# Attention and two expert layers on one core: three edits around the first pass of the routed experts

## Chip, core and metric

The kernel runs on one core of one Trainium2 chip. The metric is the time of one execution in microseconds (us), as the device measures it, with the median of three runs as the kernel's time. Engines are named as in the profile: PE (TensorE, the matmuls; its weight loads are PEld), DVE (VectorE), ACT (ScalarE), POOL (GpSimd) and SP (SyncE, which here only issues DMAs).

## What is computed

Causal attention over 2 batches of 12 heads (448 tokens of 64 each) gives a matrix x of 896 tokens by 768. A dense layer follows, x @ w_in, a gate h * sigmoid(1.702 h), then @ w_out. Then every token goes to one of 8 experts:

```python
logits = x @ w_gate
e_idx = np.argmax(logits, axis=1)
...
gate_w = probs[np.arange(N), e_idx]
eom = 1.0 / (1.0 + np.exp(-(x @ w_output_gate)))
...
for e in range(E):
    mask = e_idx == e
    h = np.maximum(x[mask] @ w1[e], 0.0)
    ye = h @ w2[e]
    out[mask] = gate_w[mask, None] * eom[mask, e, None] * ye
```

N is 896, D is 768, an expert's inner size is 1024. All inputs are float32.

## The kernel before, in words

The attention and the dense layer fill the first 392 us. Each matmul of the dense and the expert layers is done as a product of split numbers: a float32 weight tile `raw` is cast by ACT to a rounded part `hi`, and DVE makes the rest `lo = raw - hi`. PE then adds hi*hi, hi*lo and lo*hi.

**Expert passes.** A pass (`block`, line 858) takes up to 128 tokens of one expert. It has 12 steps `u`. In steps 0 to 5 (`l1`) PE multiplies the tokens `xh`, `xl` by two 128-row pieces of w1, in steps 6 to 11 (`l2m`) it multiplies the hidden values `hh`, `hl` by pieces of w2: steps with `u % 3 == 2` work on the output's last 256 columns (`pyB`), the others on its first 512 (`pyA`). Between them stand `relu` (ACT, writes `hs`), `tr` (PE transposes `hs`, ACT copies the result to `hh`, DVE makes `hl`), and at the end two scalings by ACT into `ys`, which POOL scatters to the output. `prep` (line 691) makes the next pass's `xh`, `xl` from its gathered tokens `xw`: six transposes on PE, two casts on ACT, two subtractions on DVE.

**Splits.** Each step's weights stand in one of 24 places of 512 KB and are split by `split` (line 292: one ACT cast of some 1.04 us and one DVE subtraction of some 1.22 us) into one of 6 entries, in the order of passes and steps. Five splits (`SPLIT_AT`, line 133) are done while the dense layer's last tile still runs. So at step u of a pass, `split` works on step u + 5, and from u = 7 on the next pass's weights. An entry can be written again when PE is done with the step that used it six splits earlier. When a split of a pass marked `True` in `passes` is done, SP issues the load of the same step's weights of the expert two later (`again`, line 274, `load32`, line 269). Pass 0 is marked `False`: passes 0 and 1 both use expert 0's weights, so pass 0's own splits issue no load. SP issues its DMAs in program order and stands still at the first one whose wait is not fulfilled.

**Where pass 0 and pass 1 get their tokens.** Tokens are sorted into lists in DRAM (`xl_d`), by expert. For each tile of 128 tokens, `logits` and `logits_sum` give the logits, `pick` (line 643) finds the expert and the gate weight, and `place` (line 667) computes each token's position in its expert's list and has POOL scatter the entry `lst[:, t, :]` (token number and gate weight) there. After the first five of seven tiles (`CUT`) the list of expert 0 is read and its tokens are gathered: this is pass 0. The last tile's logits, `pick` and `place` are done inside pass 0. Then POOL reads the rest of expert 0's list (`rest_lists`, line 788: `le0` and the window lists `lwin`), gathers those tokens (`first_x`, line 936), and `prep` makes them ready for pass 1. From pass 1 on the next pass's tokens are gathered early in the pass before.

**Hooks.** `block` is given functions by place: a pair such as (0, 3) runs inside or after an `l1` step of half 0 (an odd second number: after the step that holds that k), a number 6 to 11 after that step's `split`. A function's instructions are queued on each engine at that place of the program, and each engine works in program order.

The program runs 8 experts plus expert 0's second pass, then as many further passes as overfull lists need: twelve passes ran in this execution. After line 939 (the call for pass 0) every other pass is `some(p)`.

## Time and profile before

| | us |
|---|---|
| runs | 633.08, 633.17, 637.72 |
| median | 633.17 |
| the profiled execution | 635.76 |
| its span, first to last instruction | 634.0 |
| PE busy in the span | 592.1 (93%) |
| DVE busy | 470.1 (74%) |
| ACT busy | 372.1 (59%) |
| mean granted clock of PE | 0.978 of full speed |

A row of the timeline gives the start and the duration in us, the engine, the line of the program, the operation, what it writes and reads, shapes, how many instructions were merged, and in square brackets how long the engine was idle before and which event ended that. Pass 0 begins at 393.92 us of the span, pass 1 at 424.97 us, pass 2 at 444.40 us.

### The profile page before, as it was taken

Reading aid. Unit: us, or ns where it says so; the run is one execution under the profiler, and the core shown is the slowest. Engines: PE = TensorE matmul, PEld = TensorE weight load, DVE = VectorE, ACT = ScalarE, POOL = GpSimd, SP = SyncE. Lnnn points to the kernel's source line nnn. Section 1 sums busy time; section 2 is a strip of 40 time slices with the busy share of each in tenths; the row PEclk is TensorE's granted clock in tenths of the full one; section 3 lists DMA queues with packets and bytes.
Section 4 is the critical chain, followed back from the end, with each engine's and each line's share of the span. In section 5 each row is a group of like instructions: output and inputs, shape, how many; then the busy total and the mean of one; then the engine's idle time right before and its main releaser. Section 6 shows DMA issues by size and latency. Waiting matters only on the chain. (4 is left out here: it accounts for less than half of the span.)

```text
span 634.0 us, 10087 instructions
## 1 busy us (share of the span) xinstructions
PE 592.1 (93%) x3326; PEld 477.9 (75%) x3326; DVE 470.1 (74%) x890; ACT 372.1 (59%) x729; POOL 202.4 (32%) x291
## 2 busy tenths in 40 slices
PE   6999999999999979787999999959999999999995
PEld 4666666688888859687877777747888888888884
DVE  2767877467777786877844457839998888898896
ACT  3888888333333324434332225737888888888885
POOL 3354444334333343757400012230551111011110
PEclk8999999999999979998999999979999999999998
DMA  6835552125444443402592305148999999999950
GB/s 138 244 85 142 115 120 62 55 68 144 135 134 138 140 148 100 150 17 81 162 348 36 131 17 174 53 154 273 353 365 353 360 335 383 380 382 381 382 191 20
DMA packets 93144, 118.02 MB, mean 186 GB/s; under 512 B 40206, under 2 KB 53406, under 8 KB 93088
## 3 DMA queue, kind: packets, MB, share of 16 engines
q1 hardware_dynamic: 88560, 109.05, 53.3%
q0 software_dynamic: 2512, 5.54, 2.5%
q10 hardware_dynamic: 2016, 2.75, 1.2%
q8 instruction: 28, 0.46, 0.4%
q14 instruction: 28, 0.23, 0.1%
HBM read 114.10 MB, written 7.54 MB: 192 GB/s over the span
## 5 line engine op out<-in xcount | busy, mean ns | idle before, releaser
L575 PE MATMUL py<-slotA,gs 128*128 128x256 f32 (+1 forms) x609 | 115.2, 343 | 1.3 <-POOL gs L507 1.3
L575 PEld LDWEIGHTS py<-slotA,gs 128*128 128x128 f32 x609 | 93.4, 196 | 14.4 <-issue 2.7
L437 PE MATMUL ph<-xhi,slotA 128*128 128x512 f32 (+1 forms) x384 | 97.5, 373 | 4.7 <-DVE g L536 4.7
L228 POOL TENSOR_TENSOR slotA<-w,slotA 128x512 fp32r<-128x512 f32 x45 | 62.0, 1379 | 81.7 <-ACT slotA L226 81.6
L437 PEld LDWEIGHTS ph<-xhi,slotA 128*128 128x128 f32 x384 | 70.8, 191 | 15.3 <-issue 5.8
L226 ACT CAST slotA<-w 128x512 fp32r<-128x512 f32 x45 | 27.9, 620 | 89.9 <-DVE w L224 89.9
L301 DVE TENSOR_TENSOR ent<-wraw,ent 128x1024 fp32r<-128x1024 f32 x48 | 58.0, 1221 | 4.9 <-ACT ent L300 4.9
L437 PE MATMUL ph<-xlo,slotA 128*128 128x512 f32 x192 | 56.0, 372 | 0.0
L367 PE MATMUL sc<-kT,qz 128*128 128x64 f32 (+6 forms) x168 | 52.6, 397 | 3.0 <-ACT kT L358 2.8
L507 DVE TENSOR_TENSOR gs<-g,gs 128x512 fp32r<-128x512 f32 x38 | 31.5, 837 | 31.8 <-ACT gs L505 31.8
L390 POOL TENSOR_SCALAR P<-P,rc 128x64 f32<-128x64 f32 (+2 forms) x72 | 36.7, 511 | 54.4 <-DVE rc L389 40.5
L875 PE MATMUL ps_h<-ent,xh 128*128 128x512 f32 x192 | 53.9, 402 | 0.0
L224 DVE SCALAR_TENSOR_TENSOR w<-raw,w 128x512 uint32<-128x512 uint32 x46 | 51.9, 1129 | 1.2
L381 ACT ACTIVATE P<-sc,nmax 128x64 f32<-128x64 f32 (+6 forms) x84 | 40.3, 480 | 18.7 <-DVE nmax L379 7.6
L300 ACT CAST ent<-wraw 128x1024 fp32r<-128x1024 f32 x48 | 49.9, 1051 | 0.4 <-ACT y L597 0.4
L379 DVE TENSOR_REDUCE nmax<-sc 128x1 f32<-128x64 f32 (+6 forms) x84 | 34.6, 416 | 16.6 <-PE sc L368 16.4
L536 DVE TENSOR_TENSOR g<-ph,g 128x256 f32<-128x256 f32 x64 | 23.6, 389 | 30.1 <-ACT g L535 30.1
L505 ACT CAST gs<-g 128x512 fp32r<-128x512 f32 x56 | 33.1, 617 | 14.7 <-PE py L575 9.1
L875 PEld LDWEIGHTS ps_h<-ent,xh 128*128 128x128 f32 x192 | 35.0, 188 | 7.3
L398 PE MATMUL ps_pT<-ident,P 128*128 128x128 f32 x192 | 37.7, 289 | 2.2 <-POOL P L390 1.6
L301 DVE TENSOR_TENSOR ent<-wrb,ent 128x1024 fp32r<-128x1024 f32 x30 | 36.3, 1222 | 4.7 <-ACT ent L300 4.2
L221 DVE SCALAR_TENSOR_TENSOR w<-raw,w 128x512 uint32<-128x512 uint32 x46 | 38.0, 827 | 1.6
(190 smaller groups left out, 1211.8 us busy)
## 6 DMA issues: line engine op xcount, KB each, us to landing
wraw<-in_moe_w_dram SPq DMA_DIRECT2D x66, 512.0 KB, 7.8
wrb<-in_moe_w_dram SPq DMA_DIRECT2D x48, 512.0 KB, 8.2
wr<-in_moe_w_dram SPq DMA_DIRECT2D x30, 512.0 KB, 6.2
raw<-in_moe_w_in_dram SPq DMA_DIRECT2D x24, 512.0 KB, 4.3
raw<-in_moe_w_out_dram SPq DMA_DIRECT2D x22, 512.0 KB, 3.6
qraw<-in_q_dram SPq DMA_DIRECT2D x24, 112.0 KB, 2.9
kraw<-in_k_dram SPq DMA_DIRECT2D x24, 112.0 KB, 2.9
vraw<-in_v_dram SPq DMA_DIRECT2D x24, 96.0 KB, 2.5
```

The costliest lines, as they stand in the source:

```text
L221: nc.vector.scalar_tensor_tensor(wu, r[:, :, 1], 0xC0000000, wu, op0=ALU.bitwise_and, op1=ALU.bitwise_or)
L224: nc.vector.scalar_tensor_tensor(wu, r[:, :, 0], 29, wu, op0=ALU.logical_shift_right, op1=ALU.bitwise_or)
L228: nc.gpsimd.tensor_sub(slot[:, 1], w, slot[:, 0].bitcast(F32))
L300: nc.scalar.copy(hi, raw)
L301: nc.vector.tensor_sub(lo, raw, hi.bitcast(F32))
L367: nc.tensor.matmul(sc[:, :n], qT[:, j].rearrange("d h p -> d (h p)"), kT[:, :n], start=True, stop=False)
L381: nc.scalar.activation(Pb[j][:, :n], sc[:, :n], AF.Exp, bias=nm, scale=1.0, accum_out=sm)
L390: eng[NORM_ENG[j]].tensor_scalar(Pb[j][:, :n], Pb[j][:, :n], rc, 1.0, op0=ALU.mult, op1=ALU.mult)
L398: nc.tensor.transpose(ps[:, c].rearrange("p h q -> p (h q)"), Pb[j][:, c * KC:(c + 1) * KC], ident)
L437: nc.tensor.matmul(p[:, 0:128 * nt], wt, xt[:, kk, 128 * t0:128 * (t0 + nt)], start=kk == 0 and n == 0, stop=kk == KD - 1 and n == 2)
L575: nc.tensor.matmul(py[:, :n], gt[:, kk % 4], wt, start=kk == 0 and m == 0, stop=kk == KF - 1 and m == 2)
L875: nc.tensor.matmul(hps[hf], xh[:, k0 + n], wt[:, n], start=k0 + n == 0 and m == 0, stop=False)
```

## The change

Four things change, all for pass 0:

1. `pick` of the last tile stops after the expert is known (`split_off=True`). The seven operations for the gate weight move to `weigh`, which `place` calls after it has computed the positions and before the scatter. For the other tiles the order stays.
2. `block` takes a number of splits for each step (`rate`). Pass 0 has none in steps 0 to 2, two each in steps 3 to 5, one each after that. All passes keep twelve.
3. `prep` for pass 1 moves from the hook after step 10 to the one after step 11.
4. `first_x` issues, behind the gather of pass 1's tokens, a DMA of one element of `xw` to DRAM on SP's queue (`gate`), which can be issued only when the gather has landed.

```diff
--- before.py
+++ after.py
@@ -640,7 +640,7 @@
 
         ohs = {}
 
-        def pick(t):
+        def pick(t, split_off=False):
             logits_sum(t)
             lg = lg_t.pop(t)
             nm = mp.tile([128, 8], F32, name="nm", tag="nm", bufs=2)
@@ -655,6 +655,15 @@
             nc.vector.tensor_scalar(nm[:, 2:3], nm[:, 0:1], -1.0, None, op0=ALU.mult)
             nc.scalar.activation(tmp[:, 1], lg[:, 0:NE], AF.Exp, bias=nm[:, 2:3], scale=1.0,
                                  accum_out=nm[:, 4:5])
+            if not split_off:
+                weigh(t, nm, tmp, lg, ohb)
+            else:
+                late_w.append((t, nm, tmp, lg, ohb))
+            ohs[t] = ohb
+
+        late_w = []
+
+        def weigh(t, nm, tmp, lg, ohb):
             nc.vector.tensor_mul(tmp[:, 2], lg[:, NE:2 * NE], ohb)
             nc.vector.tensor_reduce(nm[:, 3:4], tmp[:, 2], axis=AX.X, op=ALU.add)
             nc.scalar.activation(nm[:, 5:6], nm[:, 3:4], AF.Exp, scale=-1.0)
@@ -662,7 +671,6 @@
             nc.vector.tensor_scalar_add(nm[:, 5:6], nm[:, 5:6], 1.0)
             nc.vector.tensor_mul(nm[:, 6:7], nm[:, 4:5], nm[:, 5:6])
             nc.vector.reciprocal(lst[:, t, 1:2], nm[:, 6:7])
-            ohs[t] = ohb
 
         def place(t):
             ohb = ohs.pop(t)
@@ -675,6 +683,8 @@
             nc.vector.tensor_mul(tmp, p[:, 0:NE], ohb)
             nc.vector.tensor_reduce(pos, tmp, axis=AX.X, op=ALU.add)
             nc.vector.tensor_copy(pos_i, pos)
+            while late_w:
+                weigh(*late_w.pop())
             nc.gpsimd.indirect_dma_start(
                 out=xl_d[:, :], out_offset=bass.IndirectOffsetOnAxis(ap=pos_i.bitcast(U32), axis=0),
                 in_=lst[:, t, :].bitcast(I32), in_offset=None, bounds_check=NT * NE - 1, oob_is_err=False)
@@ -855,7 +865,7 @@
 
         npass = [0]
 
-        def block(lw, hooks):
+        def block(lw, hooks, rate=(1,) * NU):
 
             o, last = passes[npass[0]]
             p0 = npass[0]
@@ -906,7 +916,8 @@
                 l1(u)
                 if u % 3 == 2:
                     relu(u // 3)
-                split()
+                for _ in range(rate[u]):
+                    split()
             hook("b")
             pyA = ps.tile([128, 512], F32, name="ps_yA", tag="acc", bufs=4)
             pyB = ps.tile([128, 512], F32, name="ps_yB", tag="acc", bufs=4)
@@ -924,7 +935,8 @@
                     nc.scalar.activation(ys[:, 0:512], pyA, AF.Copy, scale=scl)
                 if u == 11:
                     nc.scalar.activation(ys[:, 512:768], pyB[:, 0:256], AF.Copy, scale=scl)
-                split()
+                for _ in range(rate[u]):
+                    split()
                 hook(u)
             nc.gpsimd.indirect_dma_start(
                 out=out[:, :], out_offset=bass.IndirectOffsetOnAxis(ap=lw[:, 0:1].bitcast(U32), axis=0),
@@ -933,13 +945,16 @@
         engs = (ET.PE, ET.DVE, ET.Pool, ET.Activation, ET.SP)
         lists = [lw0, le0] + [lwin[:, e] for e in ORDER[1:]] + lo_t
 
+        gate = dram.tile([1, 1], F32, name="gate")
+
         def first_x():
             gather(le0, xw)
+            nc.sync.dma_start(gate, xw[0:1, 0:1])
 
         block(lw0, {
-            (0, 1): lambda: tr_y(TT - 1, "A"), (0, 2): last_logits, (0, 3): lambda: pick(TT - 1),
+            (0, 1): lambda: tr_y(TT - 1, "A"), (0, 2): last_logits, (0, 3): lambda: pick(TT - 1, True),
             (0, 5): last_place, (1, 0): rest_lists, (1, 3): first_x, (1, 4): counts, 6: further_constants,
-            10: lambda: prep(xw)})
+            11: lambda: prep(xw)}, (0, 0, 0, 2, 2, 2, 1, 1, 1, 1, 1, 1))
         nov = None
 
         def some(p):
```

On DVE, from the last tile's gate weight to the first `hl` of pass 0. Before (L301 is the subtraction of `split`, L675 to L677 are the positions, L892 is `hl`; L658, L659 and L661 stand ahead of these rows):

```order
L662 TENSOR_SCALAR nm<-nm 128x1
L663 TENSOR_TENSOR nm<-nm 128x1
L664 RECIPROCAL lst<-nm 128x1
L301 TENSOR_TENSOR entb<-wraw,entb 128x1024
L675 TENSOR_TENSOR tmp_4518<-ps_rk,ohb 128x8
L676 TENSOR_REDUCE pos<-tmp_4518 128x1
L677 CAST pos_i<-pos 128x1
L301 TENSOR_TENSOR entb<-wraw,entb 128x1024
L301 TENSOR_TENSOR ent_4300<-wraw,ent_4299 128x1024
L892 TENSOR_TENSOR hl<-ps_hT,hh 128x512
```

After the change (the positions are now L683 to L685, the gate weight L667 to L673, `hl` L902):

```order
L683 TENSOR_TENSOR tmp_4508<-ps_rk,ohb 128x8
L684 TENSOR_REDUCE pos<-tmp_4508 128x1
L685 CAST pos_i<-pos 128x1
L667 TENSOR_TENSOR tmp<-ps_lg,ohb 128x8
L668 TENSOR_REDUCE nm<-tmp 128x1
L670 TENSOR_SCALAR nm<-nm 128x1
L671 TENSOR_SCALAR nm<-nm 128x1
L672 TENSOR_TENSOR nm<-nm 128x1
L673 RECIPROCAL lst<-nm 128x1
L301 TENSOR_TENSOR ent_4343<-wraw,ent_4342 128x1024
L301 TENSOR_TENSOR entb<-wraw,entb 128x1024
L902 TENSOR_TENSOR hl<-ps_hT,hh 128x512
```

The subtraction that stood between the gate weight and the positions is gone, as is one that stood ahead of the logits; both, and the one behind the positions, now follow the gate weight in one row.

On PE, the end of pass 0 and the begin of pass 1. Before (L899 and L901 are `l2m`, L696 the transposes of `prep`, L875 and L879 `l1` of pass 1):

```order
L901 MATMUL ps_yA<-ent_4332,hl 128x512 x2
L696 MATMUL ps_x<-ident,xw_2992 128x128 x6
L899 MATMUL ps_yB<-ent_4342,hh 128x256
L899 MATMUL ps_yB<-ent_4343,hh 128x256
...
L901 MATMUL ps_yB<-ent_4342,hl 128x256 x4
L875 MATMUL ps_h_4686<-entb,xh 128x512 x4
L879 MATMUL ps_h_4686<-entb,xl 128x512 x2
```

After the change:

```order
L911 MATMUL ps_yA<-ent_4332,hl 128x512 x2
L909 MATMUL ps_yB<-ent_4342,hh 128x256
L909 MATMUL ps_yB<-ent_4343,hh 128x256
...
L911 MATMUL ps_yB<-ent_4342,hl 128x256 x4
L706 MATMUL ps_x<-ident,xw_2992 128x128 x6
L885 MATMUL ps_h_4688<-entb,xh 128x512 x4
L889 MATMUL ps_h_4688<-entb,xl 128x512 x2
```

The six transposes of pass 1's tokens have moved behind the twelve matmuls of step 11, directly ahead of pass 1's first step.

On SP, the last weight loads ahead of pass 0 and the first ones inside it. Before:

```order
L272 DMA wraw<-in_moe_w_dram 128x2x512 [waits DMAHW1_49,PE_49]
L272 DMA wraw<-in_moe_w_dram 128x2x512 [waits DMAHW2_49,PE_49,Pool_49]
L272 DMA wraw<-in_moe_w_dram 128x4x256 [waits DMAHW3_49,PE_49,Pool_49]
L272 DMA wr_3651<-in_moe_w_dram 128x2x512 [waits DMAHW5_49,DVE_49]
L272 DMA wr_3653<-in_moe_w_dram 128x2x512 [waits DMAHW6_49,DVE_49]
```

After the change:

```order
L272 DMA wraw<-in_moe_w_dram 128x2x512 [waits DMAHW1_49,PE_49]
L272 DMA wraw<-in_moe_w_dram 128x2x512 [waits DMAHW2_49,PE_49,Pool_49]
L272 DMA wraw<-in_moe_w_dram 128x4x256 [waits DMAHW3_49,PE_49,Pool_49]
L952 DMA gate<-xw_2992 1x1 [waits DMAHW5_49,DMASW3_49]
L272 DMA wr_3651<-in_moe_w_dram 128x2x512 [waits DMAHW6_49,DVE_49]
L272 DMA wr_3653<-in_moe_w_dram 128x2x512 [waits DMAHW7_49,DVE_49]
```

The DMA of `gate` waits for the software DMA's semaphore (the gather), and the loads that pass 0's last five splits issue stand behind it.

## Rows read from the trace of the kernel before

**Rows 1.** Stretches: us, busy (instructions) of PE, PEld, DVE, ACT, POOL, clock, DMA, GB/s

```profile
425.00:445.00 20.00, 19.43 (x102) 16.10 (x102) 16.74 (x28) 15.86 (x21) 2.52 (x2) 0.98 0.77 247
521.00:540.00 19.00, 19.00 (x103) 16.07 (x102) 16.89 (x18) 15.55 (x21) 2.96 (x3) 1.00 1.05 383
```

**Rows 2.** Timeline of PE, pass 0 to the begin of pass 1

```profile
400.16 0.18 PE L670 MATMUL ps_rk<-ohb,sut 128*128 128x8 bf16 x1
...
402.59 0.66 PE L889 MATMUL ps_hT<-ident,hs 128*128 128x128 f32 x4 [0.72 <-ACT hs L883]
...
421.10 1.51 PE L696 MATMUL ps_x<-ident,xw 128*128 128x128 f32 x6 [7.51 <-DMA xw<-y_d,le]
...
426.68 1.09 PE L875 MATMUL ps_h<-entb,xh 128*128 128x512 f32 x4
...
428.08 1.09 PE L875 MATMUL ps_h<-ent,xh 128*128 128x512 f32 x4
```

**Rows 3.** Waits, 386 to 426 us: us in total, times, longest

```profile
PEld ps_lg L638 <- DVE lT L633: 0.5, 1, 0.5
```

**Rows 4.** Timeline of DVE in pass 0

```profile
401.52 0.17 DVE L664 RECIPROCAL lst<-nm 128x1 f32<-128x1 f32 x1
402.08 1.23 DVE L301 TENSOR_TENSOR entb<-wraw,entb 128x1024 fp32r<-128x1024 f32 x1 [0.39 <-ACT entb L300]
...
403.61 0.15 DVE L677 CAST pos_i<-pos 128x1 int32<-128x1 f32 x1
...
404.83 1.22 DVE L301 TENSOR_TENSOR ent<-wraw,ent 128x1024 fp32r<-128x1024 f32 x1
405.96 0.68 DVE L892 TENSOR_TENSOR hl<-ps_hT,hh 128x512 fp32r<-128x512 f32 x1
406.57 1.22 DVE L301 TENSOR_TENSOR ent<-wraw,ent 128x1024 fp32r<-128x1024 f32 x1
...
407.97 1.23 DVE L301 TENSOR_TENSOR ent<-wraw,ent 128x1024 fp32r<-128x1024 f32 x1
```

**Rows 5.** Timeline of ACT in pass 0

```profile
401.02 1.03 ACT L300 CAST entb<-wraw 128x1024 fp32r<-128x1024 f32 x1
401.95 0.59 ACT L883 ACTIVATE hs<-ps_h 128x512 f32<-128x512 f32 x1
402.44 1.04 ACT L300 CAST entb<-wraw 128x1024 fp32r<-128x1024 f32 x1
...
413.62 0.69 ACT L924 ACTIVATE hs<-ps_yA,lw 128x512 f32<-128x512 f32 x1 [1.59 <-PE ps_yA L901]
```

**Rows 6.** Timeline of POOL: scatter of the last list, its rest, pass 1's tokens

```profile
404.04 1.73 POOL L678 DMA_INDIRECT xl_d<-lst,pos_i  x1 [9.80 <-DVE pos_i L677]
...
409.36 1.90 POOL L724 DMA_INDIRECT le<-xl_d,ix  x1 [3.47 <-DMA xl_d<-lst,pos_i]
...
413.46 1.81 POOL L686 DMA_INDIRECT xw<-y_d,le  x1 [1.22 <-issue]
```

**Rows 7.** DMA issues: count, KB where known, us from issue to landing

```profile
lo<-xl_d,ix POOLq DMA_INDIRECT x6, 6.5
...
xw<-y_d,lw POOLq DMA_INDIRECT x1, 4.6
le<-xl_d,ix POOLq DMA_INDIRECT x1, 3.3
...
xw<-y_d,le POOLq DMA_INDIRECT x1, 7.5
```

**Rows 8.** Timeline of SP's queue: weight loads after pass 0's splits

```profile
412.09 16.24 SPq L272 DMA_DIRECT2D wr<-in_moe_w_dram  x5
```

**Rows 9.** Timeline of PE in the dense layer, after a pause

```profile
268.77 0.64 PE L627 MATMUL ps_lT<-yT,wg 128*32 128x128 f32 x4 [2.34 <-DVE yT L617]
```

**Rows 10.** Stretches of one us, PE: busy (instructions), clock, DMA share, GB/s

```profile
268.00:269.00 1.00, 0.23 (x4) 0.82 0.48 193
425.00:426.00 1.00, 1.00 (x5) 0.67 0.00 0
```

## Prediction, written before the changed kernel ran

> **What bounds the kernel now.** I read the waits of PE first, then stretches of the span, then the timelines of PE, DVE, ACT, POOL and SP around pass 0. From pass 1 on PE is the bound: it is busy 19.43 of 20 us in pass 1 and 19.00 of 19 in a later stretch, where DVE has 16.89, ACT 15.55 and the granted clock is 1.00 [rows 1]. So whatever moves the begin of pass 1 moves the end by as much, as long as nothing new is late behind it. The one long wait of PE near the edits is ahead of pass 1: 7.51 us until pass 1's tokens landed [rows 2]. PE stood still from 413.59, came back at 421.10 at the lower of its two clock levels (1.2 of 2.4 GHz), and the clock rose within the microsecond 425 to 426, which has a mean of 0.67, so about 425.7 [rows 10]. The first step of pass 1 that ran at full clock begins at 426.68, and one step takes 428.08 - 426.68 = 1.40 us [rows 2]. **At full clock pass 1 would thus have begun at 426.68 - 1.40 = 425.28**; against this I count.
>
> The wait is the end of a chain: positions done (DVE, 403.61), scatter issued (404.04), landed and the rest of the list read (409.36), tokens gathered (413.46) [rows 4, 6], landed 7.5 us later [rows 7].
>
> **The change, part by part: the tokens.** Between the gate weight (ends 401.52 + 0.17 = 401.69) and the positions stand a wait of 0.39 for ACT and a subtraction of `split` that holds DVE 1.14 us [rows 4]. Both go: the last of the nine small operations starts at 403.61 - 1.53 = 402.08. Further ahead, the subtraction of step 0 leaves too. It held the logits' add, for which PE's next weight load waited 0.5 us [rows 3]; PE has own work in half of that, so I take 0.24 (bounds 0 and 0.5). Putting the positions ahead of the gate weight is worth nothing by itself: the scatter sends the token number and the gate weight together, so it starts behind both in either order. It only fills time in which DVE waits for ACT's exponential; I take 0.2 (0 to 0.5). Last operation: 402.08 - 0.24 - 0.2 = 401.64; the scatter follows 0.43 later as before [rows 4, 6]: 402.08, **1.96 us earlier** (1.5 to 2.5). From there I keep the distances, 5.32 us to the list and 4.10 us to the gather [rows 6], since nothing else moves data there: gather issued at 411.50.
>
> It took 7.5 us while SP issued five weight loads from 412.09 on [rows 8]. Now those stand behind `gate`. What a quiet queue gives isn't in the trace for this gather. The nearest rows: the list read takes 3.3 us here and 6.5 in the loaded passes, 3.2 us apart; pass 0's gather took 4.6 [rows 7]. I take 7.5 - 3.2 = 4.3, close to that 4.6; bounds are 3.3 and the old 7.5. **Tokens land at 415.8** (414.8 to 419.0), not at 421.0.
>
> **DVE.** The three splits that leave steps 0 to 2 come back in steps 3 to 5. ACT's `relu` of the first half no longer waits behind a cast that ran from 401.02 to 401.95 [rows 5]; it starts some 0.1 us behind the exponential of the gate weight, at 401.14, 0.81 earlier. The first cast follows 0.49 later (402.44 - 401.95), and its subtraction 1.06 after that (402.08 - 401.02) [rows 4, 5]: DVE starts its splits at 402.69. From there it has seven of pass 0 and five of pass 1, two `hl` and the counts, without a pause: a subtraction holds it 405.96 - 404.83 = 1.13 us, an `hl` 0.61, the counts 407.97 - 406.57 - 1.13 = 0.27 [rows 4]. That is 12 x 1.13 + 2 x 0.61 + 0.27 = 15.05 us, to 417.74. So DVE becomes the tight engine of pass 0; before, it had those three splits out of the way early.
>
> **PE.** The transposes of the first half move with `relu`, from 402.59 [rows 2] to 401.78. Then come 0.4 for them, steps 4 and 5 (1.5 each), 6, 7, 8 (1.4 each), transposes of the second half (0.35) and the first four of the six matmuls of step 9 (two thirds of 1.40, 0.93): 410.8. These are estimates from the step of 1.40 and from 0.66 for four transposes, of which the next work hides a part [rows 2]. There the second `hl` is wanted, which stands behind seven subtractions, the first `hl` and the counts: 402.69 + 7.91 + 0.61 + 0.27 + 0.68 = 412.16. **A new wait of 1.4 us.** Then 0.5, and steps 10 and 11 with 1.4 and 1.5: PE is done with pass 0 at 415.6. Step 11 is so taken ahead of the wait; before, it ran behind it, at half clock.
>
> **Begin of pass 1.** Tokens (415.8) and PE (415.6) meet. But `prep` now stands behind the scaling and the split of step 11 on ACT: scaling at 415.95 (some 0.35 behind PE; the scaling of step 10 started 0.03 behind PE's end [rows 2, 5], so this is the cautious end), cast at 416.3, first cast of `xh` 0.95 later (401.95 - 401.02 = 0.93 for a cast [rows 5]), done 417.75. PE starts at 417.8; on DVE the last subtraction starts at 417.36, the first `xl` is ready at 419.05, and PE wants it 0.93 us into the step: 0.3 us of waiting. Effective begin 418.1. The tokens have 0.9 us to spare.
>
> **The sum:** 425.28 - 418.1 = 7.2 us. From the profiled execution's 635.76 that gives 628.6; it lies 2.59 above the median of the runs, so I forecast 633.17 - 7.2 = **626.0**. Costed at nothing: the DMA of `gate` itself (one element; SP has only loads behind it); the loads it holds, four or five of the five in rows 8, until about 416.5. They are pass 3's weights, so all of pass 1 (19.43 us) and more covers them; if that cover were gone, the splits would wait, and PE behind them, as long as the hold lasts, some 4.5 us.
>
> **Rivals.** *The clock falls in the new pauses.* A pause of 2.34 us was enough in the dense layer [rows 9]: the granted clock's mean in that microsecond was 0.82 [rows 10], between the two levels. Here there are 1.4 us at 411 and 2.2 at 416, the latter broken by six transposes. Against it: each is shorter than 2.34. Before, the low level lasted from 421.10 to 425.7, 4.6 us; at half rate that costs 2.3, part of it in the pause; I take 1.8. Gain 5.4, time **627.8**.
>
> *The gather stays at 7.5.* Pass 0's gather had loads beside it and took 4.6 [rows 7]; that the other one was slow because of loads is not shown. It would land at 419.0, after a pause of 3.4, so with the clock down: first `xh` 1.4 us later as before, 420.5, and half rate until 4.6 us after the restart, 423.7, loses 1.6. Effective begin 422.1, gain 3.2, time **630.0**. The Trainium skill, "DMA: Bandwidth & Descriptors", section "Queues, rings and completion order", speaks for this one: an engine takes turns between the queues that have work, a packet at a time, so a gather should not stand behind whole loads of SP's queue, and holding them back would buy little. The list reads of 3.3 and 6.5 us [rows 7] rather agree with a queue that is waited for; I give the rule less weight than these.
>
> *DVE and ACT are less tight.* Then PE's 415.6 decides, plus some 1.1 for the first three transposes and a cast, 416.7: gain 8.6, time **624.6**.
>
> *Slower.* The held loads come as one burst when pass 2's gather is issued, and the DMA engines never catch up: in the later stretch they are full (share 1.05, 383 GB/s [rows 1]). A load is 0.524 MB, 1.37 us at 383 GB/s. If each of the ten gathers of passes 2 to 11 landed one load too late for PE, that costs 13.7 against the gain of 7.2: **639.7**. It decides from 0.72 us a pass. Against it: in pass 1 the share is 0.77 with 247 GB/s [rows 1]; the spare 136 GB/s take in four loads (2.1 MB) in 15 us, less than a pass.
>
> **How the numbers follow.** Forecast 0.50 (its own range 624.9 to 627.1: the scatter's bounds and a few tenths of waiting), clock 0.18, gather 0.14, less tight 0.08, gain lost in small waits (around 632) 0.04, slower 0.06. The range runs from 623.8, below the case with the least waits, to 630.3, above the slow gather. A measurement here tells about 1% from no change; 1% faster is below 626.84. That holds for most of the forecast's case (0.43), the less tight one (0.08) and the cheap end of the clock's (0.03): 0.54. Slower 0.06, the rest 0.40.
>
> **What would show it.** The scatter at about 402.1; the gather's landing in 4 to 5 us; a wait of PE for `hl` at step 9 of 1 to 2 us; no wait of PE for the tokens above 1 us; pass 1 begins at 417 to 418.5 at clock 1.00; DVE without a gap from 402.7 to 419; pass 1 and later as long as before. The forecast is wrong if the gather's time does not fall, if the clock is 0.5 in pass 1's first steps, or if PE waits in later passes.

## The result

The changed kernel takes 629.13 us (median of 7 runs, 628.62 to 629.49); the kernel before took 635.85 us beside it (7 runs, 633.08 to 637.72). The ratio is 0.9902 with a 95% interval of 0.9878 to 0.9925, that is 4.8 to 7.8 us of 635.85. The forecast was 626.0, range 623.8 to 630.3: the time lies inside, 3.1 us above the forecast, and the gain is just short of the 1% to which I had given 0.54.

Span to span, the profiled executions stand at 634.0 and 626.8 us: 7.2 us, the size that was forecast. Nearly all of it arises in pass 0. From pass 0's first matmul to the begin of pass 1 at full clock it was 425.28 - 393.92 = 31.36 us; now it is 24.27. From pass 2's first matmul to the end it was 634.0 - 444.40 = 189.6 us; now it is 626.8 - 437.21 = 189.6.

PE's timeline of the changed kernel, from step 9 of pass 0 to the second step of pass 1 (L909 and L911 are `l2m`, L706 the transposes of `prep`, L885 and L889 `l1`):

```profile
412.02 0.74 PE L911 MATMUL ps_yA<-ent,hl 128*128 128x512 f32 x2 [1.19 <-DVE hl L902]
...
415.38 0.82 PE L706 MATMUL ps_x<-ident,xw 128*128 128x128 f32 x6
417.53 1.20 PE L885 MATMUL ps_h<-entb,xh 128*128 128x512 f32 x4 [1.33 <-ACT xh L708]
418.88 0.73 PE L889 MATMUL ps_h<-entb,xl 128*128 128x512 f32 x2
419.44 1.09 PE L885 MATMUL ps_h<-entb,xh 128*128 128x512 f32 x4
```

The pause of 7.51 us [rows 2] is gone. In its place stand 1.19 us for `hl` at step 9 and 1.33 us for `xh`. The tokens are not waited for. Pass 1's first step starts at 417.53; its last two matmuls come 0.4 us late (418.88 instead of 417.53 + 0.93), so the second step starts at 419.44 and the begin at full clock is 419.44 - 1.40 = 418.04.

The clock in that stretch (PE busy, granted clock, DMA share, GB/s):

```profile
411.00:412.00 1.00, 0.00 (x0) 1.00 0.00 0
...
416.00:417.00 1.00, 0.20 (x2) 1.00 0.39 45
417.00:418.00 1.00, 0.47 (x2) 1.00 0.80 268
418.00:419.00 1.00, 0.85 (x5) 1.00 0.94 346
```

It stays at 1.00 through both pauses. In the kernel before it had fallen to 0.50 inside the long one:

```profile
419.00:420.00 1.00, 0.00 (x0) 0.50 1.06 407
```

POOL, DVE, ACT and SP of the changed kernel, as rows 4 to 6 and 8 show them of before, and the gather of pass 1's tokens among the DMA issues:

```profile
402.42 0.98 POOL L688 DMA_INDIRECT xl_d<-lst,pos_i  x1 [8.29 <-DMA xl_d<-lst,pos_i]
...
406.85 1.75 POOL L734 DMA_INDIRECT le<-xl_d,ix  x1 [3.34 <-DMA xl_d<-lst,pos_i]
...
410.90 1.39 POOL L696 DMA_INDIRECT xw<-y_d,le  x1 [1.32 <-PE ps_yA L909]
```

```profile
401.37 0.16 DVE L673 RECIPROCAL lst<-nm 128x1 f32<-128x1 f32 x1
402.41 1.27 DVE L301 TENSOR_TENSOR ent<-wraw,ent 128x1024 fp32r<-128x1024 f32 x1 [0.87 <-ACT ent L300]
...
411.28 0.68 DVE L902 TENSOR_TENSOR hl<-ps_hT,hh 128x512 fp32r<-128x512 f32 x1
...
418.27 1.02 DVE L709 TENSOR_TENSOR xl<-ps_x,xh 128x384 fp32r<-128x384 f32 x2
```

```profile
400.75 0.20 ACT L669 ACTIVATE nm<-nm 128x1 f32<-128x1 f32 x1 [0.78 <-DVE nm L668]
400.86 0.58 ACT L893 ACTIVATE hs<-ps_h 128x512 f32<-128x512 f32 x1
...
416.05 1.04 ACT L300 CAST ent<-wr 128x1024 fp32r<-128x1024 f32 x1
416.99 0.87 ACT L708 CAST xh<-ps_x 128x384 fp32r<-128x384 f32 x2
```

```profile
415.04 0.31 SPq L952 DMA_DIRECT2D gate<-xw  x1
415.45 3.30 SPq L272 DMA_DIRECT2D wr<-in_moe_w_dram  x5
```

```profile
xw<-y_d,le POOLq DMA_INDIRECT x1, 4.1
```

Step by step: the gate weight's last operation (L673) starts at 401.37; the scatter at 402.42 [404.04 in rows 6]; the gather at 410.90 [413.46]; it lands 4.1 us later [7.5 in rows 7], and SP's `gate` follows at 415.04 with the five loads behind it. DVE starts the first split (L301) at 402.41 and comes to the second `hl` (L902) only at 411.28, to pass 1's `xl` (L709) at 418.27. ACT casts `xh` (L708) at 416.99, directly behind the cast of the last split at 416.05.

### The profile page after: what moved, and what is told of

Its sections match the earlier page's. It is cut to its first block, busy times and chain, and to the rows that moved or that the text cites. A ratio compares the mean times of both kernels' runs of the same rounds, so it can differ in the third digit from the quotient of the medians.

```text
span 626.8 us, 10089 instructions
## 1 busy us (share of the span) xinstructions
PE 590.7 (94%) x3326; PEld 476.2 (76%) x3326; DVE 470.1 (75%) x890; ACT 371.3 (59%) x729; POOL 200.3 (32%) x291
## 5 line engine op out<-in xcount | busy, mean ns | idle before, releaser
L301 DVE TENSOR_TENSOR ent<-wraw,ent 128x1024 fp32r<-128x1024 f32 x48 | 58.0, 1222 | 5.7 <-ACT ent L300 5.7
L885 PE MATMUL ps_h<-ent,xh 128*128 128x512 f32 x192 | 54.0, 402 | 0.0
L224 DVE SCALAR_TENSOR_TENSOR w<-raw,w 128x512 uint32<-128x512 uint32 x46 | 52.0, 1131 | 1.2
L300 ACT CAST ent<-wraw 128x1024 fp32r<-128x1024 f32 x48 | 49.8, 1050 | 0.0
L885 PEld LDWEIGHTS ps_h<-ent,xh 128*128 128x128 f32 x192 | 35.0, 188 | 7.6 <-DVE ent L301 0.4
L301 DVE TENSOR_TENSOR ent<-wrb,ent 128x1024 fp32r<-128x1024 f32 x30 | 36.3, 1222 | 4.7 <-ACT ent L300 4.2
L437 PEld LDWEIGHTS ph<-xlo,slotA 128*128 128x128 f32 x192 | 35.5, 191 | 4.7
```

The lines of the kernel that those rows point to most:

```text
L224: nc.vector.scalar_tensor_tensor(wu, r[:, :, 0], 29, wu, op0=ALU.logical_shift_right, op1=ALU.bitwise_or)
L300: nc.scalar.copy(hi, raw)
L301: nc.vector.tensor_sub(lo, raw, hi.bitcast(F32))
L437: nc.tensor.matmul(p[:, 0:128 * nt], wt, xt[:, kk, 128 * t0:128 * (t0 + nt)], start=kk == 0 and n == 0, stop=kk == KD - 1 and n == 2)
L885: nc.tensor.matmul(hps[hf], xh[:, k0 + n], wt[:, n], start=k0 + n == 0 and m == 0, stop=False)
```

## The experiments

Executions differ in when pass 0 begins (393.4 to 395.4 us in the profiles below), which lies ahead of everything that the change touches. So the kernels are compared by the time from pass 0's first matmul to pass 2's first matmul, in each kernel's profile; "gather" is pass 1's gather, from issue to landing. Medians and ratios are those of the timed runs, against runs of the kernel before on the same chip; different kernels ran on different chips, so two medians are compared only where the text says that the chip was the same.

| kernel | pass 0 | pass 2 | between | gather | median | ratio to before, interval |
|---|---|---|---|---|---|---|
| before | 393.92 | 444.40 | 50.48 | 7.5 | 635.85 | |
| changed | 393.77 | 437.21 | 43.44 | 4.1 | 629.13 | 0.9902, 0.9878 to 0.9925 |
| changed, no hold | 394.21 | 437.58 | 43.37 | 4.2 | 628.84 | 0.9928, 0.9900 to 0.9956 |
| changed, `prep` at step 10 | 393.92 | 436.49 | 42.57 | 4.6 | 627.89 | 0.9907, 0.9882 to 0.9933 |
| changed, gate weight first | 393.38 | 436.43 | 43.05 | 4.1 | 628.48 | 0.9925, 0.9899 to 0.9952 |
| changed, even splits | 395.17 | 439.34 | 44.17 | 4.8 | 630.79 | 0.9961, 0.9943 to 0.9978 |
| before + hold | 394.38 | 441.73 | 47.35 | 4.4 | 632.88 | 0.9988, 0.9968 to 1.0009 |
| before + `prep` at step 11 | 394.42 | 441.34 | 46.92 | 5.5 | 632.88 | 0.9982, 0.9956 to 1.0008 |
| before + positions first | 394.26 | 441.64 | 47.38 | 6.0 | 632.93 | 0.9973, 0.9948 to 0.9998 |
| before + splits moved | 395.02 | 437.26 | 42.24 | 4.4 | 628.64 | 0.9923, 0.9900 to 0.9945 |
| changed, other numbers of splits | 395.35 | 436.96 | 41.61 | 3.9 | 627.69 | 0.9907, 0.9873 to 0.9942 |
| the same, gate weight first, no hold | 393.54 | 434.80 | 41.26 | 4.2 | 627.75 | 0.9904, 0.9876 to 0.9932 |
| changed + second hold | 394.26 | 437.61 | 43.35 | 4.1 | 628.88 | 0.9916, 0.9883 to 0.9949 |
| before + one split earlier | 393.97 | 441.31 | 47.34 | 5.8 | 634.50 | 1.0008, 0.9986 to 1.0029 |

Where no landing is printed, the table has another time. With the hold it is the time from the gather's issue to that of `gate` on SP, which elsewhere follows the landing by 0.1 us or less (410.57 to 415.17 with `prep` at step 10, 413.57 to 418.36 with even splits). For "before + splits moved" it is the time from the issue at 411.72 to PE's transposes at 416.12, for which PE waited.

One thing has to be kept in mind with the first row: the profiled execution of the kernel before, with 635.76 us, is slow for its kind: four sets of 10 to 21 runs of it have medians of 633.38 to 634.07. Four kernels whose runs differ from those of before by 0.3% or less (hold, late `prep`, positions first, one split earlier) have 46.92 to 47.38 us in this column, not 50.48. So differences to 50.48 probably overstate what an edit gives.

The theory from the prediction: the token chain comes forward, the hold makes the gather short, and then DVE's and ACT's row of splits binds pass 1. The rivals: the gather is short for another reason; the single edits do nothing or harm.

### The changed kernel without the hold

```diff
             gather(le0, xw)
-            nc.sync.dma_start(gate, xw[0:1, 0:1])
```

> The changed kernel without the DMA of gate, so the loads of pass 0's last five splits are issued as soon as their places are free. In the changed kernel the tokens land at 415.0 us and the first cast of xh starts at 417.0, so the tokens have some 1.5 us to spare. Theory A (loads slow a gather only while both are in flight): the first of these loads is issued behind the subtraction that ends at about 413.1, 1 us after the gather's descriptors are written; the gather takes 4.1 to 5.5 us, pass 1 begins where it did, time within 0.5 us of the changed kernel. Theory B (the hold is what makes the gather short): 7.5 us, tokens at 418.4, first xh near 419.4, pass 1's effective begin 420 or later: 2 to 4 us slower than the changed kernel.

SP's queue, POOL's gather and its landing:

```profile
413.54 5.63 SPq L272 DMA_DIRECT2D wr<-in_moe_w_dram  x5
```

```profile
411.28 1.44 POOL L696 DMA_INDIRECT xw<-y_d,le  x1 [2.41 <-PE ps_yA L909]
```

```profile
xw<-y_d,le POOLq DMA_INDIRECT x1, 4.2
```

The gather is as short without the hold, 4.2 us, and the stretch is 43.37 us against 43.44. The first load is issued at 413.54, 0.8 us behind the end of POOL's instruction for the gather (411.28 + 1.44 = 412.72). In the kernel before three of the five loads were issued ahead of that end: it was at 413.46 + 1.81 = 415.27 [rows 6], the first load at 412.09 [rows 8]. So once the splits are moved, no load stands ahead of the gather for the hold to keep back. Both sides have moved: counted from pass 0's first matmul, the end of the gather's instruction came 2.84 us sooner than in the profile of before (18.51 against 21.35), the first load 1.16 us later (19.33 against 18.17). Theory A.

### The kernel before with the hold alone

```diff
             gather(le0, xw)
+            nc.sync.dma_start(gate, xw[0:1, 0:1])
```

> The kernel before with the DMA of gate behind pass 1's gather and nothing else of the change. From the first matmul of pass 0 to pass 1's begin at full clock (second step minus 1.40) the kernel before takes 31.36 us, the changed one 24.27; without the hold the changed one also takes 24.26. Theory A (here the five loads are in flight with the gather, from 412.09 on, so the hold matters where the splits stay): the gather takes 4.1 to 4.8 instead of 7.5, PE's pause shrinks to 4 to 4.7 us, the clock still falls as the pause is over 2.3: 27.5 to 28.5 us, 3 to 4 us faster than before. Theory B (an engine takes turns between queues, loads do not hold a gather up): the gather stays near 7.5, no change.

PE's wait for the tokens with the second step of pass 1, the gather on POOL, and its landing:

```profile
418.47 1.51 PE L696 MATMUL ps_x<-ident,xw 128*128 128x128 f32 x6 [4.50 <-DMA xw<-y_d,le]
...
424.07 1.10 PE L875 MATMUL ps_h<-entb,xh 128*128 128x512 f32 x4
```

```profile
413.92 1.81 POOL L686 DMA_INDIRECT xw<-y_d,le  x1 [1.22 <-issue]
```

```profile
xw<-y_d,le POOLq DMA_INDIRECT x1, 4.4
```

With the splits left where they were, the hold does shorten the gather, to 4.4 us: it was issued 19.54 us behind pass 0's first matmul and its instruction took 1.81 us, both as in the profile of before [rows 6], so the loads are what differs. Pass 1 begins at 424.07 - 1.40 = 422.67, 28.29 us behind pass 0's first matmul. So far it is as theory A said, but the 3 to 4 us do not show in the runs: their ratio is 0.9988, with 1 inside its interval. The profile of before shows 3.1 us more than this one, the medians 1.2 us more. I come back to that.

### The kernel before with the splits moved alone

```diff
-        def block(lw, hooks):
+        def block(lw, hooks, rate=(1,) * NU):
...
-                split()
+                for _ in range(rate[u]):
+                    split()
...
-            10: lambda: prep(xw)})
+            10: lambda: prep(xw)}, (0, 0, 0, 2, 2, 2, 1, 1, 1, 1, 1, 1))
```

> The kernel before with pass 0's splits moved (none in steps 0 to 2, two in 3 to 5) and nothing else: gate weight ahead of the positions, prep behind step 10, loads not held. Theory A (moving the splits alone takes the loads behind the gather and the tokens forward; the other three edits give nothing or cost): tokens 21.1 to 21.6 us behind pass 0's first matmul, pass 1 at 23.0 to 23.4 us (before 31.36, changed kernel 24.27, with prep at step 10 23.47, with the gate weight first 23.91): 8.0 to 8.4 us faster than before, 0.9 to 1.3 faster than the changed kernel. Theory B (the edits need each other): 25 us or more, slower than the changed kernel.

PE, step 9 of pass 0 to pass 1's first step (L901 is `l2m`, L696 `prep`, L875 `l1`):

```profile
412.89 0.74 PE L901 MATMUL ps_yA<-ent,hl 128*128 128x512 f32 x2 [1.20 <-DVE hl L892]
...
416.12 0.84 PE L696 MATMUL ps_x<-ident,xw 128*128 128x128 f32 x6 [1.10 <-DMA xw<-y_d,le]
...
418.21 1.08 PE L875 MATMUL ps_h<-entb,xh 128*128 128x512 f32 x4
```

In the profiles this one edit shortens the stretch by 50.48 - 42.24 = 8.24 us, all four together (the title counts three) by 50.48 - 43.44 = 7.04: on top of it, the other three cost 1.2 us. The runs say less than 8.24 us for the one edit, 0.9923 or 4.9 us of 634.07, and so do the 46.92 to 47.38 us of the kernels that run like before: 4.7 to 5.1 us. Tokens land 416.12 - 395.02 = 21.1 us behind pass 0's first matmul, and pass 1 begins 23.18 behind it, as expected of theory A. By the medians the two kernels cannot be told apart (628.64 and 629.13, and they did not run side by side).

### The changed kernel with `prep` back behind step 10

```diff
-            11: lambda: prep(xw)}, (0, 0, 0, 2, 2, 2, 1, 1, 1, 1, 1, 1))
+            10: lambda: prep(xw)}, (0, 0, 0, 2, 2, 2, 1, 1, 1, 1, 1, 1))
```

> The changed kernel with prep of pass 1 back at the hook after step 10. Theory A (the new bound of pass 1's begin is the row of splits on ACT and DVE in front of prep): xh is cast ahead of the last split; PE waits some 1.1 us for the tokens (415.0), then transposes and step 11 (1.4) run, pass 1's effective begin is 417.1 instead of 418.04: 1.0 us faster than the changed kernel. Theory B (taking step 11 ahead of the wait is worth its 1.4 us): 0.5 to 1.5 us slower than the changed kernel.

```profile
415.29 0.85 PE L706 MATMUL ps_x<-ident,xw 128*128 128x128 f32 x6 [1.05 <-DMA xw<-y_d,le]
...
417.39 1.10 PE L885 MATMUL ps_h<-entb,xh 128*128 128x512 f32 x4
```

PE now waits 1.05 us for the tokens in front of step 11, and still pass 1 begins 417.39 - 393.92 = 23.47 us behind pass 0's first matmul instead of 24.27: `xh` and `xl` are made while step 11 runs, ahead of the last split. The late `prep` costs 0.87 us in the stretch to pass 2; the runs agree, with 627.89 us against 628.84 of the changed kernel without the hold on the same chip. Theory A.

### The kernel before with `prep` behind step 11 alone

```diff
-            10: lambda: prep(xw)})
+            11: lambda: prep(xw)})
```

> The kernel before with prep of pass 1 behind step 11 and nothing else. Theory A: where the tokens are 7 us late, step 11 (1.5 us at full clock, 2.7 at half) is taken into the pause; PE waits 6.0 instead of 7.5 us, the clock still falls; pass 1's begin at full clock 29.5 to 30.6 us behind pass 0's (31.36 before): 0.8 to 1.9 us faster than before. So the same edit that costs 0.8 us in the changed kernel gains where the pause is long. Theory B (prep late costs its 0.8 us everywhere): 0.5 to 1 us slower than before.

```profile
418.66 1.51 PE L696 MATMUL ps_x<-ident,xw 128*128 128x128 f32 x6 [3.31 <-DMA xw<-y_d,le]
...
422.83 1.87 PE L875 MATMUL ps_h<-entb,xh 128*128 128x512 f32 x4
```

```profile
xw<-y_d,le POOLq DMA_INDIRECT x1, 5.5
```

The stretch is 3.56 us shorter than in the profile of before, more than either theory said, but 2.0 us of that is a gather of 5.5 instead of 7.5 us, which this edit does not touch. The clock had fallen, as the 1.87 us for four matmuls at 422.83 show (1.09 at full clock). The runs show no difference (0.9982, with 1 inside). What the edit gives by itself is not settled here.

### The changed kernel with the gate weight first

```diff
-(0, 3): lambda: pick(TT - 1, True),
+(0, 3): lambda: pick(TT - 1),
```

> The changed kernel with the gate weight ahead of the positions again. The scatter needs both in either order, and in the changed kernel it waited until 402.42 for the scatter before it to land, 0.6 us behind DVE's last operation. Theory A: no change of the scatter's start (within 0.1 us) and of the time (within 0.3 us). Theory B (the order gives 0.2 us or more): the scatter at 402.6 or later, 0.2 to 0.5 us slower.

DVE and ACT (L673 the gate weight's end, L685 the positions' end, L301 the first split, L669 the exponential, L893 `relu`):

```profile
400.65 0.16 DVE L673 RECIPROCAL lst<-nm 128x1 f32<-128x1 f32 x1
...
401.11 0.15 DVE L685 CAST pos_i<-pos 128x1 int32<-128x1 f32 x1
401.69 1.23 DVE L301 TENSOR_TENSOR ent<-wraw,ent 128x1024 fp32r<-128x1024 f32 x1 [0.43 <-ACT ent L300]
```

```profile
400.03 0.20 ACT L669 ACTIVATE nm<-nm 128x1 f32<-128x1 f32 x1 [0.43 <-DVE nm L668]
400.14 0.58 ACT L893 ACTIVATE hs<-ps_h 128x512 f32<-128x512 f32 x1
```

The stretch is 0.39 us shorter than in the changed kernel, which neither theory said: I had looked at the scatter alone. With the positions first, the exponential on ACT comes behind them, and `relu` behind the exponential: at 400.14 - 393.38 = 6.76 us behind pass 0's first matmul here, at 400.86 - 393.77 = 7.09 in the changed kernel. The first split starts 8.31 and 8.64 us behind it. DVE's row of splits then carries the 0.33 us to pass 1. It is so in all eight kernels with moved splits: `relu` at 6.75 or 6.76 us with the gate weight first, at 7.09 to 7.11 with the positions first. The scatter itself is 0.5 us earlier here (8.16 and 8.65), because it did not have to wait for the scatter before it; in three kernels with the positions first that had no such wait either it is at 8.04 to 8.06, so the order itself gives the scatter 0.1 us. PE does not wait for the tokens in either kernel.

### The kernel before with the positions first

```diff
-(0, 3): lambda: pick(TT - 1),
+(0, 3): lambda: pick(TT - 1, True),
```

(with `weigh` as in the change)

> The kernel before with the positions ahead of the gate weight and nothing else. Theory A (the order only pushes the gate weight's exponential, and with it relu and the scatter, behind a cast of split, as in the kernel with the other edits and even splits): the scatter starts 10.4 to 10.7 us behind pass 0's first matmul (10.12 before), PE waits 2 us or more for relu at the first transposes (0.72 before), pass 2 begins 50 to 52 us behind pass 0's first matmul (50.48 before; 47.5 to 49 should the gather happen on two loads instead of three): not faster than before beyond noise. Theory B (the order brings the list forward): scatter at 9.9 us or earlier, 0.2 to 0.5 us faster.

DVE (L301 the subtraction of `split`, L668 what the exponential waits for), ACT (L300 a cast of `split`, L669 the exponential, L893 `relu`), and the gather:

```profile
401.78 1.23 DVE L301 TENSOR_TENSOR entb<-wraw,entb 128x1024 fp32r<-128x1024 f32 x1 [1.42 <-ACT entb L300]
...
403.58 0.16 DVE L668 TENSOR_REDUCE nm<-tmp 128x1 f32<-128x8 f32 x1
```

```profile
400.71 1.04 ACT L300 CAST entb<-wraw 128x1024 fp32r<-128x1024 f32 x1
403.77 0.20 ACT L669 ACTIVATE nm<-nm 128x1 f32<-128x1 f32 x1 [2.02 <-DVE nm L668]
403.88 0.58 ACT L893 ACTIVATE hs<-ps_h 128x512 f32<-128x512 f32 x1
```

```profile
xw<-y_d,le POOLq DMA_INDIRECT x1, 6.0
```

The scatter starts 10.57 us behind pass 0's first matmul (10.12 before), PE waits 2.30 us for `relu` at the first transposes (0.72 [rows 2]), both as theory A said, but not for the whole of its reason: ACT's cast was done at 401.75, and ACT then stood idle for 2.02 us until DVE came to L668, behind its subtraction and the positions. For `relu` the order is a loss in either surrounding. That the stretch is nevertheless 3.1 us shorter than in the profile of before is mainly the gather again, issued 1.0 us sooner (18.51 us behind pass 0's first matmul against 19.54) and landed in 6.0 us. The ratio of 0.9973 lies below 1 by less than a third of a per cent.

### The changed kernel with even splits

```diff
-            11: lambda: prep(xw)}, (0, 0, 0, 2, 2, 2, 1, 1, 1, 1, 1, 1))
+            11: lambda: prep(xw)}, (1,) * NU)
```

> The changed kernel with one split a step in pass 0, as before. Theory A (the early part is won on the token chain and lost again on DVE): the scatter starts at 403.5 to 403.9, tokens land at 416.5 to 417, but DVE is no longer late: no wait for hl at step 9; first xh at 417 to 418, pass 1's effective begin 417.5 to 418.8: within 0.7 us of the changed kernel. Theory B (the 1.96 us of the scatter go through to the end): 1.5 to 2 us slower than the changed kernel.

```profile
405.42 0.65 PE L899 MATMUL ps_hT<-ident,hs 128*128 128x128 f32 x4 [2.30 <-ACT hs L893]
...
418.48 0.85 PE L706 MATMUL ps_x<-ident,xw 128*128 128x128 f32 x6 [0.79 <-DMA xw<-y_d,le]
```

The stretch is 0.73 us longer, at the edge of theory A, but not as it said: the scatter was 10.56 us behind pass 0's first matmul (9.7 to 10.1 expected), the tokens 23.3, because the order of the gate weight, harmless or nearly so in the changed kernel, costs PE 2.30 us for `relu` here too. `hl` was on time. So moved splits are worth 8.24 us in the profiles, some 5 us by the runs, where nothing else is changed, and 0.73 us in the profiles where the hold, the late `prep` and the order already are. The runs put the latter higher, at the size of theory B: 630.79 us against 628.84 of the changed kernel without the hold on the same chip, 1.95 us. The spans of these two profiles are 1.7 us apart, but 0.96 of that lies ahead of pass 0. Whether it is 0.7 or 2 us is therefore not settled; with either, the edits stand in for each other, and their shares do not add up.

### Other numbers of splits

```diff
-            11: lambda: prep(xw)}, (0, 0, 0, 2, 2, 2, 1, 1, 1, 1, 1, 1))
+            11: lambda: prep(xw)}, (0, 0, 0, 2, 1, 1, 1, 2, 2, 1, 1, 0))
...
-            block(lists[p], hooks)
+            block(lists[p], hooks, (2,) + (1,) * (NU - 1) if p == 1 else (1,) * NU)
```

> The changed kernel with other numbers of splits: pass 0 has 0,0,0,2,1,1,1,2,2,1,1,0 (eleven), pass 1 has two in its first step. So the second hl stands behind five instead of seven subtractions, and prep stands ahead of the last split. Theory A (pass 1's begin is bound by the splits ahead of hl and prep): no wait for hl at step 9 (1.19 us in the changed kernel), PE is done with pass 0 at 414.2, tokens at 415.0, pass 1's begin 22.3 to 22.7 us behind pass 0's, 1.6 to 2.0 us faster than the changed kernel. Theory B (DVE's row of work has to be done anyway and comes back as a wait in pass 1): pass 1 begins so early, but pass 2 begins no more than 0.5 us earlier than in the changed kernel (43.4 us behind pass 0's first matmul there).

```profile
416.40 0.85 PE L706 MATMUL ps_x<-ident,xw 128*128 128x128 f32 x6 [0.79 <-DMA xw<-y_d,le]
417.49 1.20 PE L885 MATMUL ps_h<-entb,xh 128*128 128x512 f32 x4 [0.24 <-ACT xh L708]
```

Pass 1 begins 22.55 us behind pass 0's first matmul (419.30 - 1.40 - 395.35), 1.72 us earlier than in the changed kernel, and pass 2 is 1.83 us earlier: the row of splits was the bound, and the split that is put off costs nothing in pass 1. Now PE waits 0.79 us for the tokens. Theory A.

The same with the gate weight first and no hold:

> The kernel with only two of the edits left and their numbers changed: pass 0 has 0,0,0,2,1,1,1,2,2,1,1,0 splits, pass 1 two in its first step, prep of pass 1 behind step 11; the gate weight stands ahead of the positions and no load is held. From the first matmul of pass 0 to the first of pass 2 it took 50.48 us in the kernel before, 43.44 in the changed one, 41.61 with these splits and the other two edits still in. Theory A (pass 1's begin is now bound by the tokens, which neither the order of the gate weight nor the hold moves): 41.3 to 41.8 us, that is 8.7 to 9.2 us faster than before and 1.6 to 2.1 faster than the changed kernel. Theory B (the hold or the order matter here): 42.5 us or more.

41.26 us, at the lower edge of theory A. This is the fastest of the kernels by that measure, 9.2 us below the profile of before and 2.2 below the changed kernel's; by the runs it is 0.9904 of before (0.9876 to 0.9932), and its median of 627.75 is 1.4 us below the changed kernel's, without having run beside it. On the same chip the changed kernel with a second hold (below) took 628.88.

### A second hold

```diff
-                hooks[0, 2] = lambda: gather(lists[p + 1], xw)
+                def next_x():
+                    gather(lists[p + 1], xw)
+                    if p == 1:
+                        nc.sync.dma_start(gate, xw[0:1, 0:1])
+                hooks[0, 2] = next_x
```

> The changed kernel with a second hold: behind pass 2's gather SP has to wait again until these tokens have landed, so the loads of pass 1's splits come some 3 to 5 us later. Theory A (the held loads are pass 3's and later weights and have more than a pass of time; what the DMA engines lose they catch up): from pass 0's first to pass 2's first matmul 43.2 to 43.6 us as in the changed kernel (43.44), no wait of PE over 0.7 us after pass 1's begin, the span's end as far behind pass 2's first matmul as in the changed kernel (189.6 us), within 0.3 us. Theory B (the hold is paid for later): PE waits for splits in passes 3 to 9, the end 2 us or more later.

Waits of PE from 417 us on:

```profile
PE ps_h L885 <- ACT xh L708: 1.3, 1, 1.3
PE ps_yA L911 <- DVE hl L902: 0.6, 1, 0.6
```

No new wait after pass 1's begin; 437.61 - 394.26 = 43.35 us to pass 2, and from there 627.1 - 437.61 = 189.5 to the end, 628.88 us in the runs (0.9916 of before, 0.9883 to 0.9949). Loads held twice are not paid for. Theory A.

### One load more ahead of the gather

```diff
-            10: lambda: prep(xw)})
+            10: lambda: prep(xw)}, (1, 1, 1, 1, 1, 2, 1, 1, 1, 1, 1, 0))
```

(on the kernel before, with `rate` as in the change)

> The kernel before, but pass 0 has two splits in step 5 and none in step 11, so every split from step 6 on comes a step earlier, and the loads too: one more load is issued ahead of pass 1's gather. Runs so far: no load ahead of the gather's descriptors 3.9 to 4.4 us, two ahead (prep late alone) 5.5, three (before) 7.5. Theory A (the gather stands behind the loads that are in flight when its descriptors are written): four ahead, 8.5 to 9.5 us. Theory B (the number of loads is not the cause): 7.0 to 7.8 us as in the kernel before.

```profile
xw<-y_d,le POOLq DMA_INDIRECT x1, 5.8
```

This did not make the case it was meant to make. The splits moved, but the list was read 0.4 us sooner, at 408.98 - 393.97 = 15.01 us instead of 15.44, the gather was issued 1.0 us sooner (18.58 against 19.54), and its instruction ended at 414.19: only the loads of 411.55 and 413.29 were ahead of it. Its 5.8 us speak against 8.5 as much as against 7.5. Over all kernels: with no load issued ahead of the instruction's end the gather took 3.9 to 4.8 us; with one 6.0 (the positions first), with two 5.5 and 5.8, with three 7.5. Part of that is POOL's instruction itself, which took 1.08 to 2.07 us; from its end to the landing it was 2.6 to 3.0 us with no load ahead, 4.0 with one, 3.8 and 4.2 with two, 5.7 with three. Loads ahead make it longer; that each adds the same is not borne out. The stretch is 47.34 us against 50.48 in the profile of before, and yet the runs show no difference to before (1.0008, 0.9986 to 1.0029).

## Right and wrong, step by step

**The bound: right.** PE has 19.26 of 20 us in pass 1 and 19.00 of 19 later, as before [rows 1], and everything behind pass 1's begin kept its length (stretches as in rows 1):

```profile
418.00:438.00 20.00, 19.26 (x102) 15.67 (x101) 17.12 (x30) 14.65 (x20) 1.03 (x1) 1.00 0.98 344
...
514.00:533.00 19.00, 19.00 (x103) 16.03 (x103) 16.90 (x18) 15.47 (x22) 2.84 (x3) 1.00 1.05 382
```

**The token chain: two terms off, in part against each other.** The gate weight ended 0.1 us sooner than worked out. The scatter came 0.5 us later, 8.65 us behind pass 0's first matmul instead of 8.16: POOL waited for the scatter before it, which had taken until then to land. That wait was not in my chain, but it belongs to this execution: in the other four kernels with moved splits and the positions first the scatter started at 8.04 to 8.25 us, as worked out. The list then took 4.43 us instead of the 5.32 I had kept, 0.75 of the difference because the scatter's own instruction took 0.98 us on POOL instead of 1.73 [rows 6]; the gather took 4.1 instead of 4.3. Tokens at 415.0 instead of 415.8.

**The gather: right number by luck, wrong cause.** I put the fall from 7.5 us down to the hold. The runs show that loads ahead do lengthen it (4.4 us with the hold alone against 5.5 to 7.5 without) but also that the moved splits take them out of the way by themselves (4.2 us without the hold). The step that failed is "Now those stand behind `gate`": I worked out when DVE would come to pass 1's splits, and did not set that beside the gather's issue. The rival, that loads do not hold the gather up, is refuted: it took 3.9 to 4.8 us without loads ahead, 5.5 to 7.5 with them. I had drawn it from the Trainium skill, "DMA: Bandwidth & Descriptors", section "Queues, rings and completion order", which says that an engine takes turns between queues, a packet at a time. The step from there to a gather that loads do not lengthen was mine; how the packets took turns no run here shows.

**DVE's row: right.** First split at 402.41 (402.69 forecast), a wait for `hl` of 1.19 us at step 9 (1.4), PE done with pass 0 at 415.38 (415.6), first `xh` cast at 416.99 (417.25), pass 1 at 418.04 (418.1). Two small things do not fit: the terms listed for PE up to step 9 add up to 410.7, not 410.8 (it came there at 410.83), and DVE was not without a gap, it waited 0.46 us for a cast at 415.8. The kernel with other numbers of splits shows that this row is what bound: without the wait and with the last split behind `prep`, 1.83 us less.

**The order of positions and gate weight: wrong.** I gave it 0 to 0.5 us of gain on the scatter, 0.2 in the sum. It gives the scatter 0.1 us, for which PE does not wait, and costs 0.39 in the stretch, through `relu`. The step that failed is "it only fills time in which DVE waits for ACT's exponential": I had `relu` behind that exponential in DVE's row, but did not ask when both would start in the old order, 0.33 us sooner.

**The late `prep`: wrong in sign.** I counted that step 11 is taken ahead of the wait, and saw `prep` stand behind the last split, but never priced the alternative. With the tokens nearly on time it costs 0.87 us.

**The clock: right.** Pauses of 1.19 and 1.33 us left it at 1.00.

**Where I started from: off by 2.6 us.** The difference of the spans is the forecast's 7.2. I subtracted it from the median of three runs, 633.17; the profiled execution had taken 635.76, and seven runs had a median of 635.85. From the profiled execution the forecast would have been 628.6, against 629.13. But other sets of runs of the kernel before had medians of 633.38 to 634.07 (10 to 21 runs), and one of 21 went from 631.16 to 637.44 us, while the changed kernel's seven lie within 0.9 us. So its executions lie up to 6.3 us apart, nearly as much as the change gives in the profiles. In all fourteen profiles it is 189.5 to 189.7 us from pass 2's first matmul to the end, and pass 0 begins within 2 us, so such differences lie mostly between. The kernel with only the late `prep` changed is the same as before up to the gather. In its profile the scatter and the first load stand where they stood (10.13 and 18.18 us behind pass 0's first matmul; before, 10.12 and 18.17), but the gather was issued 1.0 us sooner (18.56 against 19.54), met two loads instead of three and took 5.5 us; its runs are like those of before. This fits a kernel before whose gather mostly meets fewer loads than in the profiled execution, and whose usual loss is some 5 us rather than 7; but before itself was profiled once, so that is argued and not shown. That the spans differ by just the forecast's 7.2 us is then luck in part: it is the difference to a slow execution of before. What is shown is the ratio.

## To carry to other kernels

When work is moved out of the way of a critical chain, ask which transfers its end triggers: here moving three splits put the gather ahead of the loads (three of the five had been ahead of it in the profile of before), and the DMA that was added to hold them back then gave nothing. Before adding a second and third edit around the same wait, price each on top of the first, since they stand in for each other: from pass 0's first to pass 2's first matmul it took 42.24 us with one edit and 43.44 with all four. And an operation that only sends its result on at the end of a chain may have something queued behind it on its engine (`relu` behind the exponential) that is dearer than the chain.

## What the runs showed of the hardware

- An indirect DMA that moves little is not short: in the changed kernel's profile the seven scatters of 128 rows of 8 bytes took 3.5 to 9.3 us to land. The last of them was held up by the landing of the one ahead of it, issued at 392.37: DVE's last operation for it ended at 401.53, and it started 0.89 us later at 402.42, where in eleven of the fourteen profiles the scatter follows by 0.28 us.
- A gather's landing depends on loads issued ahead of it on another queue: 3.9 to 4.8 us with none, 5.5 to 7.5 with one to three of 512 KB.
- The granted clock stayed at 1.00 through pauses of PE of 1.19 and 1.33 us with 4.2 us of work between them, and through one of 2.30 us in the changed kernel with even splits. It fell to 0.50 inside the pause of 7.51 us, and its mean was 0.82 in the microsecond at the end of one of 2.34 us [rows 9, 10]. With the positions first, a pause of 3.52 us ended at full clock (0.85 us for six transposes, against 1.51 behind the 7.51 us), and the clock went to 0.50 only at 421, with PE at work again since 418.95. So the length of a pause alone did not tell what the clock does.
